# Dividing five groups' values by their sums after the value matmul, in a newly planned order

## The chip, the cores and the metric

The kernel runs on one core of a Trainium2 chip. The metric is the device time of one execution in microseconds (us); the number shown for a kernel is the median of three runs.

## The reference

Sparse attention in 32 heads, then a feed-forward layer on its output. S is 768, D is 64, the window 16, a block 32; there are 4 batches of 8 heads, 3072 tokens, 512 model and 2048 hidden columns.

```python
k_sum = k.reshape(B, H, nb, block, D).max(axis=3)
v_sum = v.reshape(B, H, nb, block, D).mean(axis=3)
scores_l = scale * q @ k^T, kept where |i - j| < window, else -1e9
scores_s = scale * q @ k_sum^T + log(block)
a = exp(scores_all - max);  a = a / (sum(a) + 1e-9)
attn = a @ concat(v, v_sum)
x = attn as (tokens, 512);  h = x @ w_in;  g = h * cos(h);  out = g @ w_out
```

The weights arrive in double precision, as pairs of 32-bit words, and the kernel rebuilds single precision from the bits.

## The kernel before

The 3072 tokens are eight blocks of 384. A block's attention is done in four groups, a to d, each a pair of heads; "b0" is group b of block 0. A group has six tiles of 64 queries for each of two heads, laid out as 128 rows (two half tiles) by six. Each tile sees 96 keys of its window and 24 block summaries, NK = 120 columns, so the scores of a group are 128 x 720. A column behind the 120 holds 1e-9, which the sum takes in.

Steps of a group, with the letters that the order uses: load q, k, v and the value summaries (q, k, v, m: the queue of SyncE, SP); turn q and k with PE and copy them to SBUF (tq, tk, cq, ck); key summaries (ks); masks into PSUM and scores on top (ms, sc, L556, L569); copy to SBUF (z); maximum (mx, L588, DVE); subtract it (su, L593, POOL); exponential (ex, L606, ACT); sum (sm, L609, DVE) and its reciprocal (iv, L614, DVE); multiply all exponentials by it (nm, L617, POOL); turn them with PE in two parts and copy them (tp, L626; cp); values (va, L670, PE); high part of x (xh) and what it leaves (xl, L356, DVE). From block 2 on the masks are added by DVE, and from c2 on the exponentials are turned by DVE in squares and put in place through DRAM (pt, po, pi) and not by PE.

Weights come in 16 slices w0 to w15, each 128 hidden columns: load (l), magnitude (ab, L388, ACT), clamp (cl, L393, DVE or POOL), three integer steps on DVE (sh, lb, fb, L399, L407, L415), high part (hi) and low part (lo, L356). The steps of the feed-forward part, s0 to s127, each take one block and one slice: 12 matmuls up (L714), the cosine gate on ACT and DVE, a high and a low part, 9 matmuls down (L770). s0 to s5 do block 0 with the first six slices, s6 to s21 block 1 with all, s22 to s31 the rest of block 0; then block after block. v0_0 and v0_1 are the value summaries of batch 0: load, halve (h, L259), sum (s).

The order of the instructions is written out in full as the string ORDER (lines 27 to 177): one list of tokens "who.step.banks.engine" for all engines. Each engine, and SP's queue of loads, runs its own tokens in that order and waits where an operand is not there. Buffers are few: slices share raw tiles (SLOTS) and two staging tiles, and all PSUM banks are named in the tokens.

Of the kernel before, what the change touches and what calls it, by code (L numbers as in the profile page):

```python
# [42 lines left out]
w8.sh.0.1 w3.hi.a b1.su a1.va.5 d1.z.0.v s1.tu c1.tp.0.7 w8.lb w3.lo.p a2.v d1.z.1.a c1.tp.1.3 s0.sq a2.tq.6 s1.re
c1.cp.1.a a1.xh.a s2.up.3 d1.mx s1.si c1.cp.0.a s0.ga d1.su w7.l w8.fb.0 s0.hi.a s1.sq c1.va.2 s0.lo.p w9.ab.1 s1.ga
w6.l s3.up.7 w8.hi.v s2.tu b2.q s1.hi.v d1.ex w9.cl.v s1.lo.p a1.xl s0.dh.0.1.4 s2.re w8.lo.p c1.xh.v s3.tu s0.dl
c1.xl s2.si s3.re s4.up.5 a2.cq.v v1_0.s.p d1.sm s2.sq s3.si s2.ga s1.dh w7.ab.0 d1.iv s2.hi.v d1.nm v1_1.l w9.sh.2.3
s1.dl s3.sq b1.ex s3.ga s2.lo.p d1.tp.0.6 w9.lb d1.tp.1.7 s2.dh w7.cl.p s4.tu b1.sm d1.cp.1.a s2.dl d1.cp.0.a s4.re
# [910 lines left out]
```

## Time and profile before

| | |
|---|---|
| median of 3 runs | 663.17 us (660.64 to 663.44) |
| profiled execution | 661.89 us |
| its span | 660.1 us |
| PE busy | 632.6 us (96%) |
| DVE, ACT, POOL busy | 449.7, 363.9, 221.8 us |

How to read it: a matmul record's time overlaps with the next one's, so the cost of a group of them is taken from the start of its first record to the start of what follows. A float32 matmul shows as two records. PEclk is the granted clock of PE: 1.00 is 2.4 GHz and 0.50 is 1.2 GHz. Waits name what came last before the engine went on.

### The profile page before, as it was taken

To read this page: it belongs to the slowest core of one execution; us is meant where nothing else is said; L and a number is where in the kernel's file an instruction comes from. 1 tells how busy PE (TensorE), PEld (TensorE's weight loads), DVE (VectorE), ACT (ScalarE), POOL (GpSimd) and SP (SyncE) were. 2 spreads that over 40 slices of the span, in tenths; PEclk is the share of its full clock that TensorE was granted. 3 is DMA by queue.
4 is the path that set the end of the run, shared out by engine and by line. 5 is a ranking of instruction groups with operands and counts; after the bars stand their busy time and mean duration, and the time that the engine had idled before them with its cause. 6 is when DMAs were issued, how large, how long until landed. Compare 5 with 4: busy or idle time off the path is not lost.

```text
span 660.1 us, 13282 instructions
## 1 busy us (share of the span) xinstructions
PE 632.6 (96%) x5141; PEld 560.2 (85%) x5141; DVE 449.7 (68%) x798; ACT 363.9 (55%) x640; POOL 221.8 (34%) x219
## 2 busy tenths in 40 slices
PE   6478999999999999999999999999999999999996
...
GB/s 224 259 271 203 276 15 223 169 109 71 55 122 85 91 124 132 127 59 114 111 107 135 147 98 97 114 43 85 115 163 104 92 94 70 5 1 17 16 17 48
DMA packets 167158, 72.68 MB, mean 110 GB/s; under 512 B 136824, under 2 KB 155832, under 8 KB 167096
## 3 DMA queue, kind: packets, MB, share of 16 engines
...
q8 instruction: 40, 0.66, 0.4%
q14 instruction: 22, 0.18, 0.1%
HBM read 53.72 MB, written 15.73 MB: 105 GB/s over the span
## 4 chain that ended last, share of the span: by engine, by line
PE 86%; DMA 5%; SPq 3%; POOL 2%; DVE 1%; issue 1%; ACT 1%; DVEq 0%; POOLq 0%; ACTq 0%
PE banks L770 39%; PE banks L714 39%; PE banks L569 4%; PE banks L670 3%; DMA late<-in_moe_w_out_dram 3%; DMA late<-in_v_dram 1%; SPq L456 1%; POOL w L356 1%; DMA late<-in_q_dram 1%; POOL gl L356 1%; SPq L493 1%; POOL stage L393 0%; ACT stage L388 0%; PE banks L556 0%; DVE m L588 0%
## 5 line engine op out<-in xcount | busy, mean ns | idle before, releaser
L714 PE MATMUL banks<-xh,w 128*128 128x384 f32 x1024 | 272.1, 337 | 0.1
L770 PE MATMUL banks<-w,gh 128*128 128x512 f32 x768 | 198.1, 393 | 0.2 <-ACT gh L350 0.2
L714 PEld LDWEIGHTS banks<-xh,w 128*128 128x128 f32 x1024 | 185.9, 188 | 2.8 <-ACT pt L350 0.4
L714 PE MATMUL banks<-xl,w 128*128 128x384 f32 x512 | 171.4, 335 | 0.0
L770 PEld LDWEIGHTS banks<-w,gh 128*128 128x128 f32 x768 | 142.6, 188 | 29.0 <-ACT gh L350 0.5
L724 ACT ACTIVATE t<-banks 128x384 int32<-128x384 f32 x128 | 62.5, 489 | 133.6 <-DVE gl L356 54.9
L356 POOL TENSOR_TENSOR gl<-t,gh 128x384 fp32r<-128x384 f32 x55 | 56.6, 1029 | 221.4 <-ACT gh L350 86.0
L770 PE MATMUL banks<-w,gl 128*128 128x512 f32 x384 | 109.8, 394 | 0.1
L727 DVE SCALAR_TENSOR_TENSOR t<-t,banks 128x384 f32<-128x384 int32 x128 | 70.0, 548 | 56.9 <-ACT t L724 56.2
L732 ACT ACTIVATE t<-t 128x384 f32<-128x384 f32 x128 | 66.7, 523 | 66.3 <-DVE t L727 66.0
L714 PEld LDWEIGHTS banks<-xl,w 128*128 128x128 f32 x512 | 96.1, 188 | 1.6
L739 DVE SCALAR_TENSOR_TENSOR t<-t,banks 128x384 f32<-128x384 f32 x128 | 69.3, 546 | 41.2 <-ACT t L735 41.0
L770 PEld LDWEIGHTS banks<-w,gl 128*128 128x128 f32 x384 | 71.1, 188 | 14.6 <-DVE gl L356 0.2
L593 POOL TENSOR_TENSOR sc<-sc,m 128x720 f32<-128x720 f32 x28 | 40.1, 1431 | 129.2 <-DVE m L588 129.2
L735 ACT ACTIVATE t<-t 128x384 f32<-128x384 f32 x128 | 65.8, 521 | 2.1
L617 POOL TENSOR_TENSOR sc<-sc,r 128x720 f32<-128x720 f32 x28 | 39.5, 1411 | 51.4 <-DVE r L614 50.3
L350 ACT CAST gh<-t 128x384 fp32r<-128x384 f32 x68 | 34.7, 510 | 33.2 <-PE banks L770 16.5
L356 DVE TENSOR_TENSOR gl<-t,gh 128x384 fp32r<-128x384 f32 x73 | 41.7, 572 | 12.6 <-ACT gh L350 6.5
L356 POOL TENSOR_TENSOR w<-stage,w 128x1024 fp32r<-128x1024 f32 x15 | 36.2, 2416 | 10.0 <-ACT w L350 8.6
L352 DVE CAST gh<-t 128x384 fp32r<-128x384 f32 x60 | 23.2, 386 | 22.2 <-PE banks L770 20.4
L580 DVE SCALAR_TENSOR_TENSOR sc<-banks,mask 128x360 f32<-128x360 f32 x48 | 24.4, 524 | 19.2 <-PE banks L569 19.0
L569 PEld LDWEIGHTS banks<-kd,qd 64*64 64x64 f32 x1344 | 28.4, 135 | 9.4 <-issue 6.7
(102 smaller groups left out, 620.7 us busy)
## 6 DMA issues: line engine op xcount, KB each, us to landing
...
```

Source lines behind the costliest of these rows:

```text
L350: eng.copy(out=out, in_=in_)
L356: eng.tensor_tensor(out=lo, in0=src, in1=hi.bitcast(F32), op=ALU.subtract)
L569: nc.tensor.matmul(out=self.sp[hh][s * QT : (s + 1) * QT, c, lo : lo + n], lhsT=self.qd[rows, t * QT : (t + 1) * QT], rhs=self.kd[rows, ke ...
L593: nc.gpsimd.tensor_tensor(out=self.sc, in0=self.sc, in1=self.m.unsqueeze(2).broadcast_to([P, U, NK]), op=ALU.subtract)
L617: nc.gpsimd.tensor_tensor(out=self.sc, in0=self.sc, in1=self.r.unsqueeze(2).broadcast_to([P, U, NK]), op=ALU.mult)
L714: nc.tensor.matmul(out=self.h, lhsT=w_of(name, self.f)[:, c * P : (c + 1) * P], rhs=x_of(self.blk, part, c), start=n == 0, stop=n == last,)
L724: nc.scalar.activation(out=self.t.bitcast(I32), in_=self.h, func=AF.Copy, scale=1.0 / TWO_PI)
L727: nc.vector.scalar_tensor_tensor(out=self.t, in0=self.t.bitcast(I32), scalar=-TWO_PI, in1=self.h, op0=ALU.mult, op1=ALU.add)
L732: nc.scalar.activation(out=self.t, in_=self.t, func=AF.Sin, scale=0.5)
L735: nc.scalar.activation(out=self.t, in_=self.t, func=AF.Square, scale=math.sqrt(2.0))
L739: nc.vector.scalar_tensor_tensor(out=self.t, in0=self.t, scalar=-1.0, in1=self.h, op0=ALU.add, op1=ALU.mult)
L770: nc.tensor.matmul(out=self.acc[i], lhsT=g[:, i * P : (i + 1) * P], rhs=w_of(name, self.f), start=self.first and n == 0, stop=self.last an ...
```

## The change

LATE marks five groups: a0, b0, c0, d0 and a1. For these the sum (sm) and the multiplication of all exponentials (nm) are gone. The exponentials are turned as they are, now 121 rows with the 1e-9 column (tp). The value matmuls change sides: the exponentials are the weights and the values move, so that the output has queries as rows and 64 columns for each of six pairs of tile and head; a second matmul beside each, with a column of ones as the moving side, writes the sum into a 65th column. The reciprocal is read from there (iv), DVE multiplies the values by it into a tile xq which all five share (xn), and three PE transposes bring the result back to the layout of x (tx). PMAX is empty, so what it selects is not used.

The second string of TURNS moves b2 to the way through squares and DRAM. Two clamps, w3's and w7's, go from POOL to DVE and one, w4's, from DVE to POOL, so that one is left on POOL. ORDER is new throughout; shown is the part up to the first step s0.

```diff
@@ ORDER and its constants
+PMAX = ""
+LATE = "11111000000000000000000000000000"
-TURNS = ("00000000011111111111111111111111", "00000000001111111111111111111111")
+TURNS = ("00000000011111111111111111111111", "00000000011111111111111111111111")
 ORDER = """
-b0.k a0.q a0.k c0.q c0.k b0.tk.0.0 d0.k b0.ks.0 a0.tq.1 b0.tk.1.2 v0_1.l b0.ks.1 a0.tk.0.3 a0.cq.v v0_0.l a0.tk.1.4
-b0.ck.0.v a0.ck.0.a a0.ks.0 a0.ms.5.6 a0.ck.1.a a0.ks.1 b0.q a0.sc c0.tk.0.7 a0.z.1.a a0.z.0.v w1.l c0.ck.0.a a0.mx
-d0.tk.0.1 c0.ks.0 a0.su c0.tq.0 c0.tk.1.3 d0.q c0.cq.a d0.tk.1.4 c0.ms.6.5 d0.ks.1 a0.ex v0_1.h.p c0.ks.1 c0.ck.1.v
-w0.l d0.ks.0 c0.sc a0.sm c0.v c0.z.1.a v0_0.h.v b0.tq.7 c0.z.0.a b0.ms.0.3 b0.ck.1.a a0.iv v0_0.s.p b0.cq.a v0_1.s.v
-d0.ck.0.a b0.sc w1.ab.0 c0.mx c0.m d0.tq.5 b0.z.1.a w1.cl.v c0.su d0.ms.2.1 b0.z.0.a w2.l w1.sh.6.7 d0.cq.a d0.ck.1.a
-d0.sc w1.lb a0.nm c0.ex a0.v d0.z.1.a w1.fb.1 a0.tp.0.3 d0.z.0.a a0.tp.1.0 w0.ab.0 a0.m d0.mx w1.hi.a w0.cl.v d0.su
-d0.m c0.sm w0.sh.4.5 w5.l w1.lo.p c0.iv w2.ab.0 w0.lb c1.m a0.cp.0.a w2.cl.v c0.nm d0.ex b1.q w0.fb.1 a0.cp.1.a w3.l
-a0.va.1 d0.sm w0.hi.a d1.m w2.sh.6.7 w0.lo.p c0.tp.0.2 c1.q d0.iv w5.ab.0 w2.lb b1.tq.3 a1.q a0.xh.a d0.nm c0.tp.1.0
-w2.fb.1 c0.cp.0.a d0.v c0.cp.1.a w5.cl.v w2.hi.a c0.va.2 a0.xl w2.lo.p d0.tp.0.6 c0.xh.a w5.sh.4.5 w4.l d0.tp.1.7 a1.m
-b0.mx w3.ab.0 a1.tq.0 w5.lb b0.su a1.v a1.cq.a a1.ms.1.0 w5.fb.1 w3.cl.p b0.ex b0.m d0.cp.0.a a1.sc b0.sm b1.cq.a
-c1.tq.6 d0.cp.1.a c0.xl a1.z.1.a d0.va.3 b0.iv w3.sh.4.5 b0.nm a1.z.0.a b1.m c1.ms.7.2 d0.xh.a a1.mx c1.cq.a d1.q
-w4.ab.0 c1.sc w3.lb a1.su b0.v b0.tp.0.0 w5.hi.a b0.tp.1.1 d0.xl w4.cl.v c1.z.0.a c1.v b0.cp.0.a w4.sh.6.7 c1.z.1.a
-b1.ms.3.0 b0.cp.1.a v1_0.l c1.mx a1.ex w8.l w4.lb c1.su b0.va.2 b1.sc a1.sm b0.xh.a w5.lo.p c1.ex d1.tq.1 b0.xl
-b1.z.1.a a2.q a1.iv s0.up.2 w4.fb.0 b1.z.0.a a1.nm w3.fb.1 w4.hi.a a1.tp.0.0 d1.cq.a w4.lo.v w9.l d1.ms.3.6 s0.tu
...
+b0.k a0.k v0_0.l a0.q c0.k b0.tk.0.0 d0.k a0.tk.0.1 b0.tk.1.2 c0.q a0.ck.0.a a0.ks.0 b0.ck.0.v v0_0.h.p b0.ks.0 v0_1.l
+b0.ks.1 a0.tq.3 a0.tk.1.4 a0.ms.5.6 a0.ck.1.a a0.ks.1 b0.q v0_0.s.p a0.cq.v b0.ck.1.v a0.sc w1.l c0.tk.0.7 a0.z.1.a
+a0.z.0.v c0.tk.1.1 a0.mx c0.ck.1.a d0.q c0.ck.0.v a0.su c0.tq.0 c0.ks.1 d0.tk.0.4 c0.cq.a d0.tk.1.3 w0.l d0.ck.0.v
+c0.ms.2.6 a0.ex c0.ks.0 v0_1.h.p d0.ks.0 c0.sc a0.v d0.ks.1 b0.tq.5 b0.ms.1.0 b0.cq.a v0_1.s.v c0.z.0.a c0.z.1.a
+a0.tp.0.7 a0.tp.1.2 b0.sc a1.q w1.ab.0 c0.mx w2.l d0.tq.6 w1.cl.v c0.su d0.cq.a w1.sh.4.5 d0.ck.1.a b0.z.0.a d0.ms.6.3
+a0.cp.0.a w1.lb d0.sc a0.m w0.ab.0 w1.fb.1 d0.z.1.a c0.m a0.cp.1.a w0.cl.v d0.z.0.a w1.hi.a d0.mx w5.l w0.sh.4.5 c0.ex
+w1.lo.p c0.v w0.lb b1.q a0.va.1 d0.su w2.ab.1 w0.fb.0 c1.q w2.cl.v w0.hi.a w2.sh.2.3 d0.ex w0.lo.p c0.tp.0.7 w3.l
+a0.iv w5.ab.1 w2.lb c0.tp.1.6 d0.m c0.cp.0.a w5.cl.v c0.cp.1.a w2.fb.0 b1.tq.7 d0.v c0.va.6 a0.xn w2.hi.a w5.sh.4.5
+w4.l a0.tx.2 d0.tp.0.3 b0.z.1.a w2.lo.p a1.tq.1 d0.cp.0.a b0.mx a0.xh.a a1.ms.0.3 w5.lb b0.v a1.cq.a w3.ab.1 b0.su
+d0.tp.1.1 a1.sc a0.xl w5.fb.0 b0.m d0.cp.1.a c1.tq.2 b0.ex d0.va.1 w3.cl.v b1.cq.a w8.l a1.z.0.a c0.iv w3.sh.4.5
+a1.z.1.a c1.ms.7.0 c1.cq.a v1_0.l d0.iv w4.ab.1 a1.mx b0.tp.0.3 d1.q b0.tp.1.2 c1.sc d0.xn b0.cp.1.a w4.cl.p b1.m
+w3.lb b0.cp.0.a d0.tx.1 c1.z.0.a b0.va.2 d0.xh.a c0.xn a1.m c1.z.1.a d0.xl c0.tx.3 b0.iv b1.ms.7.6 c1.mx c0.xh.a b1.v
+w5.hi.a a1.su c0.xl b1.sc w4.sh.0.1 c1.su a1.ex c1.v d1.tq.3 b0.xn b1.z.1.a w4.lb b0.tx.2 w5.lo.p a1.tp.0.6 a1.v
+b0.xh.a d1.cq.a b0.xl c1.ex w4.fb.1 s0.up.3 w7.l b1.z.0.a v1_0.s.p w3.fb.0 w4.hi.a c1.m d1.ms.2.7 a1.cp.0.a w4.lo.v
...
@@ -305,6 +309,8 @@
     KW = WINDOW + S + WINDOW
     qd0 = const.tile([P, TB], F32, name="qd")
+    ones = const.tile([P, 1], F32, name="ones")
+    nc.vector.memset(ones, 1.0)
     kmax = const.tile([P, NB // 2, BLOCK // 2], F32, name="kmax")
     kd = [const.tile([P, KW + NB], F32, name=f"kd{i}") for i in range(NPAIR)]
     vn0 = [const.tile([NK, U, P], F32, name=f"vn{i}") for i in range(2)]
@@ -440,6 +446,10 @@
             self.squares, self.moved = (t[blk * NG + pr : blk * NG + pr + 1] == "1" for t in TURNS)
+            self.late = LATE[blk * NG + pr : blk * NG + pr + 1] == "1"
+            self.rows = NK + 1 if self.late else NK
+            self.pmax = int(PMAX[blk * NG + pr : blk * NG + pr + 1] or "0")
             self.kT, self.pT, self.pt, self.pts = {}, {}, {}, None
         def load_heads(self, t, src, squares):
@@ -549,6 +559,7 @@
         def score_banks(self, two):
             self.sp = [bank(i)[:, : QC * NK].rearrange("p (c n) -> p c n", c=QC) for i in two]
+            self.first_bank = two[0]
         def place_masks(self, *two):
             self.score_banks(two)
@@ -585,6 +596,16 @@
         def maximum(self):
             m = self.m = att.tile([P, U], F32, name="m", bufs=2)
+            if self.pmax:
+                i = self.first_bank
+                nc.vector.tensor_reduce(
+                    out=m.rearrange("p (c h) -> p h c", h=2),
+                    in_=banks[:, i : i + 2, : QC * NK].rearrange("p h (c n) -> p h c n", n=NK),
+                    axis=AX.X, op=ALU.max,
+                )
+                if self.pmax == 2:
+                    nc.vector.tensor_scalar_mul(m, m, -1.0)
+                return
             nc.vector.tensor_reduce(
                 out=m, in_=self.sc, axis=AX.X, op=ALU.min if self.fused else ALU.max
             )
@@ -595,8 +616,16 @@
             )
         def exp(self):
-            self.r = att.tile([P, U], F32, name="r", bufs=2)
-            if self.fused:
+            if not self.late:
+                self.r = att.tile([P, U], F32, name="r", bufs=2)
+            if self.pmax == 2:
+                for u in range(U):
+                    c, h = divmod(u, 2)
+                    nc.scalar.activation(
+                        out=self.sc[:, u, :], in_=self.sp[h][:, c, :], func=AF.Exp, bias=self.m[:, u : u + 1],
+                        accum_out=self.r[:, u : u + 1],
+                    )
+            elif self.fused:
                 for u in range(U):
                     nc.scalar.activation(
                         out=self.sc[:, u, :], in_=self.sc[:, u, :], func=AF.Exp, bias=self.m[:, u : u + 1],
@@ -609,7 +638,11 @@
             nc.vector.tensor_reduce(out=self.r, in_=self.all[:, :, : NK + 1], axis=AX.X, op=ALU.add)
         def inverse(self):
-            if self.fused:
+            if self.late:
+                self.r = att.tile([P, U], F32, name="r", bufs=2)
+                nc.vector.reciprocal(out=self.r, in_=self.xw[:, :, D])
+                return
+            if self.fused or self.pmax == 2:
                 nc.vector.tensor_scalar_add(self.r, self.r, 1e-9)
             nc.vector.reciprocal(out=self.r, in_=self.r)
@@ -621,15 +654,15 @@
         def turn_p(self, j, i):
             lo, hi = ((0, 4), (4, U))[j]
-            pT = self.pT[j] = bank(i)[:NK, : (hi - lo) * P].rearrange("p (t n) -> p t n", t=hi - lo)
+            pT = self.pT[j] = bank(i)[: self.rows, : (hi - lo) * P].rearrange("p (t n) -> p t n", t=hi - lo)
             for t in range(lo, hi):
-                nc.tensor.transpose(out=pT[:, t - lo, :], in_=self.sc[:, t, :], identity=ident)
+                nc.tensor.transpose(out=pT[:, t - lo, :], in_=self.all[:, t, : self.rows], identity=ident)
         def place_p(self, j, eng):
             lo, hi = ((0, 4), (4, U))[j]
             if self.pts is None:
                 self.pts = att.tile([P, U * P], F32, name="pt")
-            pt = self.pts[:NK].rearrange("p (t n) -> p t n", t=U)
+            pt = self.pts[: self.rows].rearrange("p (t n) -> p t n", t=U)
             copy(eng, pt[:, lo:hi, :], self.pT[j])
             for t in range(lo, hi):
                 self.pt[t] = [pt[:, t, s * QT : (s + 1) * QT] for s in range(2)]
@@ -662,6 +695,19 @@
         def values(self, i):
+            if self.late:
+                self.xw = bank(i)[:, : U * (D + 1)].rearrange("p (u n) -> p u n", u=U)
+                for t in range(U):
+                    c, s = divmod(t, 2)
+                    for hh in range(2):
+                        p, to = self.pt[2 * c + hh][s], self.xw[s * QT : (s + 1) * QT, 2 * c + hh]
+                        nc.tensor.matmul(
+                            out=to[:, :D], lhsT=p[:NK], rhs=self.vn[:, t, hh * D : (hh + 1) * D],
+                            start=True, stop=True,
+                        )
+                        nc.tensor.matmul(out=to[:, D:], lhsT=p, rhs=ones[: self.rows], start=True, stop=True)
+                return
             self.xps = bank(i)[:, :TB]
             for t in range(U):
                 c, s = divmod(t, 2)
@@ -671,6 +717,18 @@
                         out=self.xps[rows, t * QT : (t + 1) * QT], lhsT=self.vn[:, t, rows],
                         rhs=self.pt[2 * c + hh][s], start=True, stop=True,
                     )
+        def divide(self):
+            nc.vector.tensor_tensor(
+                out=self.xq.rearrange("p (u n) -> p u n", u=U), in0=self.xw[:, :, :D],
+                in1=self.r.unsqueeze(2).broadcast_to([P, U, D]), op=ALU.mult,
+            )
+        def turn_x(self, i):
+            self.xps = bank(i)[:, :TB]
+            for c in range(QC):
+                cols = slice(c * P, (c + 1) * P)
+                nc.tensor.transpose(out=self.xps[:, cols], in_=self.xq[:, cols], identity=ident)
         def x_part(self, part):
             return x_of(self.blk, part, self.pr)
@@ -844,7 +902,7 @@
         return got if len(shape) == 2 else got.rearrange("p (c n) -> p c n", c=shape[1])
     n_v, n_k, n_s = U * P, KC * P, U * NKP
-    x1 = [xp.tile([P, 2 * TB], F32, name=f"x1_{i}", tag=t) for i, t in enumerate(("xh01", "xl01", "xh11"))]
+    x1 = [xp.tile([P, 2 * TB], F32, name=f"x1_{i}", tag=t) for i, t in enumerate(("xh01", "xl01", "xh11", "xl11"))]
     qd1 = carve(late[2], 2 * n_k, P, TB)
     kn = [carve(late[2], 0, P, KC, P), carve(late[2], n_k, P, KC, P), carve(x1[2], 0, P, KC, P), None]
     qn = [
@@ -862,6 +920,7 @@
     for t in vn_b:
         nc.gpsimd.memset(t[:, U - 1, :], 0.0)
+    Group.xq = carve(x1[3], 0, P, TB)
     groups = [
         [Group(0, i, vn_a[i], sc[i], qn[i], kn[i], (qd0, qd1)[i % 2]) for i in range(NG)],
         [Group(1, i, vn_b[i], sc[i], qn[i], kn[i], (qd0, qd1)[i % 2]) for i in range(NG)],
@@ -905,7 +964,7 @@
             q="load_q", k="load_k", v="load_v", m="load_vs", tq="turn_q", tk="turn_k", qt="square_q", kt="square_k", pt="square_p", po="move_out", pi="move_in", cq="place_q",
             ck="place_k", ks="k_summaries", ms="place_masks", sc="scores", z="scale", mx="maximum",
             su="less_max", ex="exp", sm="sums", iv="inverse", nm="normalize", tp="turn_p", cp="place_p",
-            va="values", xh="x_high", xl="x_low",
+            va="values", xn="divide", tx="turn_x", xh="x_high", xl="x_low",
         ),
         Summaries: dict(l="load", h="halve", s="sum"),
         Slice: dict(
```

## Rows read from the trace of the kernel before

**Rows 1.** The page, parts 1 and 2: busy time, and tenths in 40 slices.

```profile
span 660.1 us, 13282 instructions
...
PE 632.6 (96%) x5141; PEld 560.2 (85%) x5141; DVE 449.7 (68%) x798; ACT 363.9 (55%) x640; POOL 221.8 (34%) x219
...
PE   6478999999999999999999999999999999999996
```

**Rows 2.** Busy time by windows: PE, PEld, DVE, ACT, POOL, PEclk, DMA share, GB/s.

```profile
0.00:10.00 10.00, 5.12 (x18) 3.89 (x19) 3.79 (x10) 2.24 (x3) 4.91 (x34) 1.00 0.88 201
10.00:20.00 10.00, 7.56 (x123) 5.39 (x123) 6.29 (x11) 4.10 (x9) 4.02 (x3) 1.00 1.06 290
...
30.00:40.00 10.00, 4.80 (x47) 3.81 (x49) 9.68 (x13) 6.45 (x10) 7.94 (x5) 0.50 0.85 245
40.00:50.00 10.00, 8.19 (x105) 5.98 (x102) 7.85 (x10) 5.36 (x11) 8.65 (x4) 0.74 0.85 230
...
22.93:58.74 35.81, 22.52 (x338) 16.30 (x337) 31.29 (x37) 22.78 (x39) 25.95 (x15) 0.76 0.80 211
```

**Rows 3.** PE's waits from 0 to 100 us: total, times, longest.

```profile
PE banks L502 <- DMA late<-in_q_dram: 6.6, 3, 2.4
PE banks L670 <- ACT pt L350: 5.6, 2, 5.4
...
PE banks L670 <- DMA vn<-in_v_dram: 2.3, 1, 2.3
```

**Rows 4.** PE in order of time: start, duration, line, records, idle time before.

```profile
11.11 1.09 PE L569 MATMUL banks<-kd,qd 64*64 64x96 f32 x48
...
56.71 0.92 PE L670 MATMUL banks<-pt,vn 120*64 120x64 f32 x24 [2.27 <-DMA vn<-in_v_dram]
...
58.88 0.43 PE L714 MATMUL banks<-xh,w 128*128 128x384 f32 x1
...
61.06 0.60 PE L626 MATMUL banks<-ident,sc 128*120 128x128 f32 x4
61.50 1.38 PE L556 MATMUL banks<-mask,ident 128*128 128x360 f32 x4
62.71 0.38 PE L626 MATMUL banks<-ident,sc 128*120 128x128 f32 x2
63.02 1.09 PE L569 MATMUL banks<-kd,late 64*64 64x96 f32 x48
64.04 0.45 PE L714 MATMUL banks<-xh,w 128*128 128x384 f32 x1
...
66.36 0.92 PE L670 MATMUL banks<-pt,late 120*64 120x64 f32 x24
67.21 0.65 PE L626 MATMUL banks<-ident,late 128*120 128x128 f32 x4
```

**Rows 5.** DVE in order of time.

```profile
22.93 0.70 DVE L393 TENSOR_SCALAR stage<-stage 128x1024 f32<-128x1024 f32 x1 [0.31 <-ACT stage L388]
...
28.80 0.90 DVE L609 TENSOR_REDUCE r<-late 128x6 f32<-128x726 f32 x1
...
30.75 0.18 DVE L614 RECIPROCAL r<-r 128x6 f32<-128x6 f32 x1
...
58.18 0.56 DVE L356 TENSOR_TENSOR xl<-banks,xh 128x384 fp32r<-128x384 f32 x1 [1.14 <-ACT xh L350]
```

**Rows 6.** POOL in order of time.

```profile
15.20 2.36 POOL L259 TENSOR_TENSOR late<-late 96x1024 f32<-96x1024 f32 x1
...
24.83 1.38 POOL L617 TENSOR_TENSOR sc<-sc,r 128x720 f32<-128x720 f32 x1
...
44.18 3.62 POOL L393 TENSOR_SCALAR stage<-stage 128x1024 f32<-128x1024 f32 x1
```

**Rows 7.** ACT in order of time: w5's magnitude.

```profile
37.20 1.15 ACT L388 ACTIVATE stage<-late 128x1024 f32<-128x1024 f32 x1 [1.99 <-DMA late<-in_moe_w_out_dram]
```

**Rows 8.** SP's queue in order of time: the first two loads of b0's v.

```profile
52.91 1.26 SPq L477 DMA_DIRECT2D vn<-in_v_dram  x2
```

More of the change, by code (lines that the diff above doesn't have):

```diff
@@ L43 @@
[L43 to L47, printed above, removed]
@@ new lines @@
+s25.ga d2.su c2.pt.0 s23.dl s25.hi.a d2.ex c2.po s24.dh s25.lo.v b3.q s27.re s24.dl s27.si s25.dh d2.sm d2.iv d2.nm
+s28.up.3 s21.ta.0.0.v s26.tu s27.sq s26.re s21.st.0 c2.pi s26.si s29.up.1 s26.sq s26.ga s27.ga s26.hi.v s30.up.2
+s26.lo.v s28.tu s28.re d2.pt.0 s28.si s25.dl s28.sq s26.dh d2.po s27.hi.a v2_0.l s27.lo.v s21.st.1 s28.ga s26.dl
+s28.hi.a a3.sc.5.0 s30.tu s28.lo.p c2.va.3 a3.z.0.v s29.tu s30.re s31.up.5 c2.xh.a d2.pi b3.qt s30.si s30.sq s30.ga
+s27.dh c3.q s29.re a3.z.1.v s29.si s27.dl s29.sq s29.ga s28.dh a3.v a3.mx s28.dl s29.hi.v a3.m s30.hi.a d2.va.2
@@ new lines @@
+s51.re s52.up.1 s50.lo.v b4.kt.1 a4.z.0.v c4.k b4.qt s53.up.3 a4.z.1.v s52.tu s51.si s52.re s47.st.2 s51.sq b4.ks.1
+s52.si a4.v s51.ga s49.dh a4.mx b4.ks.0 a4.su b4.m s49.dl s51.hi.a s52.sq b4.sc.0.6 s51.lo.v a4.ex c4.q s50.dh
+b4.z.0.v c4.kt.0 c4.kt.1 s50.dl s47.ta.1.1.a a4.sm s51.dh s53.tu d4.k a4.iv b4.z.1.v a4.nm s51.dl s52.ga s53.re
+s54.up.0 s52.hi.a a4.pt.0 s53.si b4.mx a4.po s55.up.5 c4.ks.1 b4.su s53.sq c4.ks.0 c4.qt s53.ga s56.up.6 s52.lo.v
+s53.hi.a s54.tu s53.lo.v s54.re s55.tu s52.dh s54.si s55.re a4.pi s54.sq s55.si s54.ga s52.dl b4.ex s54.hi.v s53.dh
@@ new lines @@
+d7.sc.6.1 s101.sq b7.va.2 d7.z.0.v d7.z.1.v s103.up.0 d7.m d7.mx s101.ga d7.su c7.pi s101.hi.v s104.up.6 d7.ex
+s101.lo.v s102.hi.v s105.up.1 s103.tu s103.re d7.sm s103.si s101.dh s102.lo.v s101.dl s103.sq s102.dh s105.tu b7.xh.a
+b7.xl s102.dl s103.ga c7.va.5 s105.re s106.up.2 c7.xh.a s105.si s103.hi.a s105.sq s103.lo.v s107.up.0 c7.xl s104.tu
+s104.re s104.si s104.sq s103.dh s104.ga s105.ga s103.dl s104.hi.v s105.hi.v s104.dh s104.lo.v s106.tu s105.lo.v
+s104.dl s106.re d7.iv s108.up.5 s106.si d7.nm s106.sq s107.tu s107.re s109.up.6 s106.ga s107.si d7.pt.1 s106.hi.a
```

250 lines of the change are left out of this document (120 added, 130 removed).

## The prediction

> **What bounds the kernel now.** I read the page first [rows 1]: TensorE (PE) is busy for 632.6 of 660.1 us, and its line of tenths shows where the other 27.5 us lie: in the first four slices of 16.5 us and in the last one. From the fifth slice on PE has work in every slice, so from there the kernel is a row of matmuls whose length is given, and a faster VectorE (DVE), ScalarE (ACT) or GpSimd (POOL) buys nothing there. The windows come next [rows 2]: from 30 to 40 us PE is busy for 4.80 of 10 us and its granted clock is 0.50 (1.2 GHz); DVE is busy for 9.68 in the same stretch. So the opening is held by DVE and by what feeds it, not by PE. PE's waits in the first 100 us [rows 3] are late loads of q (6.6 us), a copy of the transposed exponentials that comes late on ACT (5.6 us, 5.4 of it in one piece) and a load of v (2.3 us). Last, PE's order of time [rows 4]: the first matmul of the feed-forward part (L714, step s0) starts at 58.88 us, right behind group b0, the last of block 0 to be ready; behind it PE has next to no gap. That gives the frame: the end moves by what s0's start moves, plus PE work that is added behind s0, plus any new gap behind it, with about 5 us of copies and stores after the last matmul.
>
> **Part 1: the late division, work that goes.** In five groups (a0, b0, c0, d0, a1) the sum over the exponentials goes (DVE, L609, 0.90 us each [rows 5]) and so does the multiplication of all 720 exponentials (POOL, L617, 1.38 us each [rows 6]): 4.5 us of DVE and 6.9 of POOL. The chain of one group loses these two steps between the exponential and the transposes.
>
> **Part 1: work that comes, on PE.** A group's values (L670, 24 records) take 0.85 us, 66.36 to 67.21 [rows 4]. After the change there are 24 records more, with the same 64 columns of weights but one moving column. Lower bound: the scores (L569), 48 records with 64-column weights and 96 or 24 moving columns, take 1.02 us from 63.02 to 64.04 [rows 4], 21 ns a record, so 24 cost 0.51. Upper bound: they cost like the 64-column records, 0.85; if the new order of the halves (four records on one half of the output before the other, instead of two) also took away the overlap of the halves, the old part would go up to 24 x 57 ns = 1.37, where 57 ns is 64 columns at the rate of the masks (L556: 4 x 360 columns in 1.21 us, taken as 0.89 ns a column with its start [rows 4]). I take 0.51, since one column is nearer to 24 than to 64. Then come three transposes back: four take 0.44 us from 61.06 to 61.50 [rows 4], three 0.33. So a group costs PE 0.84 more (0.84 to 1.70), five groups 4.2 (to 8.5).
>
> The Trainium skill speaks against the cheap value: "TensorEngine Tiling (Array Packing)", Instruction Overhead, says that a matmul with one free column has the latency of one with 60. No run here shows a one-column matmul. By that rule the ones would cost 0.85 a group, four groups 1.4 us more on PE before s0, and the forecast below would be 660.2.
>
> **Part 1: work that comes, on DVE.** The division (384 numbers out of PSUM) is nearest to the x rest at L356, 0.56 [rows 5]; the reciprocal, 0.18 [rows 5], stays but moves behind the values. Upper bound for the division 0.90, the reduction over 720. So DVE gains 0.90 - 0.56 = 0.34 a group (0 to 0.34). All five groups share one buffer for the divided values (xq), so each division waits for the transposes of the one before.
>
> **Where these lie.** The work of four groups stands before s0. a1's stands behind it, on the full PE: +0.84; against it a1's first transposes move ahead of s0 (0.44) and b2's six transposes leave PE (0.66, the price of four scaled up): -0.26, to +0.6 at the upper price. b2's transposes become one DVE instruction and a round trip by five DMAs, at a place where DVE is two thirds busy over the span [rows 1] and PE has other groups and steps: 0; without that cover it is the latency of one trip. The clamp: w3 and w7 go from POOL to DVE, w4 from DVE to POOL: 3.62 us on POOL against 0.70 on DVE [rows 5, 6]. Before s0 that is one for one; behind it POOL loses a1's multiplication and one clamp, 5.0 us, and DVE gets 0.70. All else in the order counts as 0 behind s0: PE had no wait of over 0.5 us there.
>
> **Part 2: the new order, the head.** SyncE's queue now has block 0's v sums (two loads, 768 KB) before a0's q. At the 201 to 290 GB/s of the first two windows [rows 2] that is 2.6 to 3.8 us. So a0's scores, at 11.11 before [rows 4], come at about 14, and so does everything that follows in PE's order. But the first weight slice, w1, has the same loads ahead of it, so its magnitude on ACT can start when it did, and DVE's stream of slices begins when c0's maximum is done. Both steps of the first v sum are now on POOL ahead of a0's subtraction (a halving is 2.36 [rows 6]), and the sum of the other stands on DVE before c0's maximum. DVE started its stream at 22.93 [rows 5]; I take 24.1 (22.9 if the v work fits the idle time, 25.5 if most of the delay of q comes through).
>
> **The new order, DVE's floor.** From 22.93 to 58.74 DVE was busy for 31.29 us and idle for 4.52 [rows 2]. Counting both orders, this stretch loses the sums of c0, d0, b0 and a1 (3.6), gains four divisions (2.24) and one reciprocal (0.18), swaps one clamp for another: 31.29 - 1.2 = 30.1. With no idle time at all b0's last step would end at 24.1 + 30.1 = 54.2.
>
> **The new order, PE's way there.** c0's values wait for c0's copy, which stands on ACT behind w5's magnitude, which waits for w5's load (37.20 before [rows 7]). Between w0 and w5 SyncE issues 11 DMAs instead of 14, at 0.63 us each (two in 1.26 [rows 8]): 35.3. Magnitude 1.15 [rows 7] and two copies of about 0.5 give 37.3 for c0's values. From there to s0 PE has, at full clock, three values (1.36 each), four times three transposes (0.33), transposed exponentials of d0, b0 and half of a1 (1.8), three q (0.33), masks (1.21) and scores (1.02) of three groups: 4.1 + 1.3 + 1.8 + 1.0 + 3.6 + 3.1 = 14.9 us. In the old windows the clock was 0.50 from 30 to 40 and 0.74 from 40 to 50 [rows 2], about 7.5 us at 1.2 GHz behind 37.3. Time at half speed does half the work: 37.3 + 14.9 + 3.7 = 55.9. What takes away the rest of the old wait: b0's v, issued at 52.91 [rows 8] and the 2.3 us wait of [rows 3], has six load steps (13 DMAs, 8 us) less ahead of it.
>
> **The sum.** The later of 54.2 (DVE) and 55.9 (PE) is 55.9, 3.0 us before 58.88; behind s0 -0.3 to +0.6, taken as +0.1. The profiled execution took 661.89 us (its span 660.1 and 1.8 around it): 661.9 - 3.0 + 0.1 = 659.0. The median of the three runs, 663.17, is 1.3 above the profiled one, the lowest 1.3 below it.
>
> **The rivals.** (B) PE's waits vanish and DVE alone decides: the stream starts at 22.9 and runs without a gap, 53.0, so 5.9 before: 656.1. For it: DVE's four old waits for sums and POOL clamps go. Against: new waits for PE (reciprocals stand in DVE's order and wait for values). (C) Slower: PE becomes the bound of the opening at 1.2 GHz. Place: c0's values to s0. Price: half of each us at the low clock; 37.3 + 14.9 + h/2 passes 58.88 when h is over 13.4 us, that is when the clock stays low until 50.7. With h = 19 it is 61.7: 664.8. For it: PE still has its hole from about 31 to 37, in front of which the clock fell before; against: the work behind it is denser. (D) The edit does what it says, but off the path: DVE starts at 24.1, does 30.1, and is idle for 4.52 as before, now behind the reciprocals and one xq: 58.7, so 661.8.
>
> **How the numbers follow.** Forecast 0.42 (657.3 to 660.6: DVE's floor to the dear ones), B 0.22, C 0.18, D 0.18. A measurement here can tell about 0.5% from no change, 3.3 us: under 658.6 is faster, over 665.2 slower by profile, and C reaches from 663 to 670. Faster: B and 0.16 of the forecast, 0.38. Slower: most of C with gaps behind s0 added, 0.16. Same: the rest, 0.46. The range leaves out the far ends of B and C: 655.5 to 665.0.
>
> **What would show it.** Right: s0's first matmul at 54 to 57.5 us, PE full behind it; a group's values at 1.2 to 1.5 us; the division at 0.5 to 0.6; no PE wait for b0's v. Wrong in its steps: s0 at 58 or later with DVE idle in front of reciprocals or divisions (D), or with PE busy at 1.2 GHz from 38 to 55 (C); values at 1.7 or more (the dear ones); PE waits behind s0 that sum up to over 1 us (the rest of the order is not neutral).

## The result and the profile after

The median is 665.67 us after (663.59 to 667.09, 10 runs) against 663.13 before, the ratio 1.0042 [1.0028, 1.0055]: slower by a little under 3 us, and 0.7 us above the upper end of the range. The profiled execution took 666.1 us, 4.2 more than that of before; its s0 starts at 64.43 us, where 55.9 was forecast and 58.88 was the old place [rows 4]. So the sign was wrong, and in this pair of profiles all of the loss lies ahead of s0: from s0 to the end of the span it is 599.9 us after and 601.2 before.

Lines have moved with the diff: L512 (old L502) turns q, L705 and L709 are the late values and their ones, L731 the turning back, L659 (old L626) that of the exponentials, L567 and L580 masks and scores, L772 and L828 up and down, L394 (old L388) the magnitude.

The page of after, against [rows 1]:

```profile
span 664.3 us, 13551 instructions
...
PE 639.9 (96%) x5270; PEld 569.7 (86%) x5270; DVE 445.6 (67%) x791; ACT 366.1 (55%) x645; POOL 211.4 (32%) x218
```

PE has 7.3 us more of busy time and 3.1 less of idle time (24.4 against 27.5); their sum is the 4.2. The part that was meant to be the gain, less idle PE, came. The part that was priced too low, PE's own time, is larger.

Windows of after, columns as in [rows 2]; the last two are in 20 us:

```profile
30.00:40.00 10.00, 4.70 (x54) 4.52 (x54) 7.93 (x9) 4.73 (x7) 6.06 (x3) 0.67 0.96 224
40.00:50.00 10.00, 8.01 (x65) 6.90 (x65) 6.39 (x8) 5.13 (x9) 3.71 (x2) 0.50 1.17 276
50.00:60.00 10.00, 10.00 (x215) 8.63 (x214) 6.43 (x12) 6.10 (x13) 4.98 (x2) 0.98 0.95 211
60.00:80.00 20.00, 19.41 (x249) 16.62 (x248) 19.46 (x28) 17.74 (x30) 12.60 (x10) 1.00 0.95 260
80.00:100.00 20.00, 20.00 (x141) 17.03 (x140) 18.15 (x29) 16.11 (x29) 15.06 (x12) 1.00 0.40 80
```

DVE, busy for 9.68 of 10 us from 30 to 40 before, is down to 7.93, and to 6.4 in the next two windows, while PE goes up to 8.01 at a clock of 0.50 and then to 10.00. The opening has changed its bound, from DVE to PE. Behind 60 us DVE is at 97% and 91%.

PE's waits from 0 to 100 us, against [rows 3]. One of them is new, 7.0 us for value summaries ahead of a0's values, at the place where PE waited 5.4 us for ACT's copy before. (The profile names the summaries of c0, x, whose load stands right behind a0's; in the run warm below the same wait is for a0's own, vn.) The waits for q are 5.4 us in total against 6.6, but the longest is 3.4 against 2.4.

```profile
PE banks L705 <- DMA x<-vs: 7.0, 1, 7.0
PE banks L525 <- DMA late<-in_k_dram: 5.5, 2, 4.8
PE banks L512 <- DMA late<-in_q_dram: 5.4, 2, 3.4
```

PE in order of time, against [rows 4]. The fence names the first record of each step; a late group's values are alternating pieces of L705 and L709.

```profile
35.30 0.44 PE L705 MATMUL banks<-vn,pt 120*64 120x64 f32 x2 [6.99 <-DMA x<-vs]
...
42.11 0.87 PE L512 MATMUL banks<-ident,late 128*128 128x128 f32 x3 [1.99 <-DMA late<-in_q_dram]
42.91 0.48 PE L705 MATMUL banks<-x,pt 120*64 120x64 f32 x2
...
46.12 0.90 PE L731 MATMUL banks<-ident,x 128*128 128x128 f32 x3
...
52.36 0.33 PE L705 MATMUL banks<-x,pt 120*64 120x64 f32 x2
...
54.22 1.48 PE L567 MATMUL banks<-mask,ident 128*128 128x360 f32 x4
...
59.63 0.55 PE L731 MATMUL banks<-ident,x 128*128 128x128 f32 x3
60.01 1.38 PE L567 MATMUL banks<-mask,ident 128*128 128x360 f32 x4
...
64.43 0.45 PE L772 MATMUL banks<-xh,w 128*128 128x384 f32 x1 [0.52 <-ACT late L518]
```

c0's values start at 42.91 (37.3 forecast), a late group at full clock takes 1.86 us (52.36 to 54.22; 1.36 forecast) and at 1.2 GHz 3.21 (42.91 to 46.12). From 42.91 to s0 PE is idle for 0.6 us in all, so the row of its work ends in s0.

### The profile page after: what moved, and what is told of

It reads as the page before. It is cut to its first block, busy times and chain, and to the rows that moved or that the text cites. A ratio compares the mean times of both kernels' runs of the same rounds, so it can differ in the third digit from the quotient of the medians.

```text
span 664.3 us, 13551 instructions
## 1 busy us (share of the span) xinstructions
PE 639.9 (96%) x5270; PEld 569.7 (86%) x5270; DVE 445.6 (67%) x791; ACT 366.1 (55%) x645; POOL 211.4 (32%) x218
## 4 chain that ended last, share of the span: by engine, by line
PE 94%; DMA 3%; SPq 1%; POOL 1%; DVE 1%; issue 0%; ACT 0%; DVEq 0%
PE banks L772 41%; PE banks L828 40%; PE banks L580 5%; PE banks L716 3%; DMA late<-in_q_dram 2%; PE banks L567 1%; DMA late<-in_moe_w_out_dram 1%; PE banks L705 1%; PE banks L659 1%; PE banks L512 1%; SPq L466 0%; PE banks L731 0%; PE banks L709 0%; POOL late L263 0%; DVE vs L273 0%; POOL late L614 0%
## 5 line engine op out<-in xcount | busy, mean ns | idle before, releaser
L772 PE MATMUL banks<-xh,w 128*128 128x384 f32 x1024 | 272.4, 337 | 0.5 <-ACT late L518 0.5
L828 PE MATMUL banks<-w,gh 128*128 128x512 f32 x768 | 198.5, 393 | 0.0
L772 PEld LDWEIGHTS banks<-xh,w 128*128 128x128 f32 x1024 | 186.0, 188 | 3.3 <-ACT late L518 0.7
L772 PE MATMUL banks<-xl,w 128*128 128x384 f32 x512 | 171.4, 335 | 0.0
L828 PEld LDWEIGHTS banks<-w,gh 128*128 128x128 f32 x768 | 142.4, 188 | 28.7
L362 POOL TENSOR_TENSOR gl<-t,gh 128x384 fp32r<-128x384 f32 x53 | 53.8, 1016 | 200.8 <-DVE gh L358 78.0
L828 PE MATMUL banks<-w,gl 128*128 128x512 f32 x384 | 109.8, 394 | 0.0
L772 PEld LDWEIGHTS banks<-xl,w 128*128 128x128 f32 x512 | 96.1, 188 | 1.9
L828 PEld LDWEIGHTS banks<-w,gl 128*128 128x128 f32 x384 | 71.1, 188 | 14.4
L356 ACT CAST gh<-t 128x384 fp32r<-128x384 f32 x73 | 37.3, 511 | 55.7 <-DVE t L797 35.2
L650 POOL TENSOR_TENSOR sc<-sc,r 128x720 f32<-128x720 f32 x25 | 35.4, 1415 | 94.6 <-DVE r L647 75.4
L362 DVE TENSOR_TENSOR gl<-t,gh 128x384 fp32r<-128x384 f32 x75 | 41.7, 558 | 27.9 <-PE banks L828 18.4
L580 PEld LDWEIGHTS banks<-kd,qd 64*64 64x64 f32 x1344 | 28.2, 134 | 8.7 <-issue 5.9
L591 DVE SCALAR_TENSOR_TENSOR sc<-banks,mask 128x360 f32<-128x360 f32 x48 | 24.4, 523 | 16.1 <-PE banks L580 16.1
```

Of the source, the lines that this page charges most:

```text
L356: eng.copy(out=out, in_=in_)
L362: eng.tensor_tensor(out=lo, in0=src, in1=hi.bitcast(F32), op=ALU.subtract)
L580: nc.tensor.matmul(out=self.sp[hh][s * QT : (s + 1) * QT, c, lo : lo + n], lhsT=self.qd[rows, t * QT : (t + 1) * QT], rhs=self.kd[rows, ke ...
L650: nc.gpsimd.tensor_tensor(out=self.sc, in0=self.sc, in1=self.r.unsqueeze(2).broadcast_to([P, U, NK]), op=ALU.mult)
L772: nc.tensor.matmul(out=self.h, lhsT=w_of(name, self.f)[:, c * P : (c + 1) * P], rhs=x_of(self.blk, part, c), start=n == 0, stop=n == last,)
L828: nc.tensor.matmul(out=self.acc[i], lhsT=g[:, i * P : (i + 1) * P], rhs=w_of(name, self.f), start=self.first and n == 0, stop=self.last an ...
```

## The experiments

Two theories from these rows. **P**: PE's own work, dearer than priced and begun at 1.2 GHz, is the new bound of the opening. **Q**: the new order of the loads brings w2, w5, a0's summaries and q too late, so PE's row starts late. Both can hold; the runs size them. The start of c0's values and those of the first up-matmuls of s0 and s5 are of the profiled execution, the ratio is of all runs.

| kernel | c0's values | s0 | s5 | ratio to before, 95% |
|---|---|---|---|---|
| before | 39.26 | 58.88 | 84.95 | 1 |
| after | 42.91 | 64.43 | 89.42 | 1.0042 [1.0028, 1.0055] |
| late_old | 44.21 | 67.48 | 93.41 | 1.0129 [1.0091, 1.0168] |
| order_only | 49.85 | 82.03 | 108.04 | 1.0353 [1.0326, 1.0380] |
| no_ones | 42.58 | 59.87 | 85.37 | 1.0030 [1.0009, 1.0050] |
| warm | 41.95 | 60.63 | 90.50 | 1.0038 [1.0011, 1.0066] |
| warm_a2q | 41.06 | 59.38 | 85.58 | 1.0032 [1.0013, 1.0052] |
| q_first | 40.74 | 61.86 | 88.28 | 1.0029 [1.0010, 1.0049] |
| loads | 39.53 | 60.61 | 87.66 | 1.0050 [1.0033, 1.0067] |
| loads2 | 40.65 | 60.23 | 86.76 | 1.0019 [1.0004, 1.0034] |
| loads3 | 38.09 | 59.16 | 85.75 | 1.0034 [1.0017, 1.0052] |
| before_b0v | 41.21 | 59.26 | 86.18 | 1.0013 [0.9997, 1.0029] |
| before_warm | 39.18 | 59.75 | 85.27 | 1.0017 [0.9999, 1.0034] |
| before_both | 40.13 | 58.81 | 88.54 | 1.0032 [1.0015, 1.0049] |

**Each half alone: late_old and order_only.** late_old is the changed kernel in the order of before, with TURNS as before and iv, xn and tx put in ahead of each late group's xh; order_only keeps the new order and makes no group late.

```diff
late_old:   ORDER = that of before; -a0.sm -a0.iv -a0.nm  +a0.iv +a0.xn +a0.tx.1 (ahead of a0.xh; b0, c0, d0, a1 alike)
order_only: -LATE = "11111000..."  +LATE = "00000000..."  +a0.sm +a0.iv +a0.nm (ahead of a0.tp; the others alike)
```

> The late division alone, in the order of the kernel before: for a0, b0, c0, d0, a1 the sum and the multiplication are taken out, and reciprocal, division and transposes back stand right ahead of the copy to x; loads, b2 and clamps as before. Theory P (PE is the bound of the opening, and the added PE work, 1.0 us of ones and 0.3 to 0.5 us of transposes a group at full clock, double at 1.2 GHz, makes s0 late): s0 at 62 to 65 us instead of 58.9, 665 to 668 us. Theory Q (the new order of the loads makes s0 late; the added work fits PE's idle time): s0 at 58 to 60, 661.5 to 664.

> The new order alone: no group divides late; for the five groups sum, reciprocal and multiplication stand ahead of the transposes of the exponentials, and the copy to x right behind the values. Theory P: PE's opening is 5 to 8 us shorter, s0 at 58 to 60, 659 to 662 us. Theory Q: the loads are as late as in the changed kernel, s0 at 62 to 65, 664 to 668 us.

The late division in the order of before costs 1.3% and puts s0 at 67.48, later than either theory had it; c0's values start at 44.21, 5 us later than before. So the new order isn't the cause of the loss as a whole: it takes back two thirds of what the late division costs in the old one. How much of the 1.3% comes from an order that wasn't planned for it is not shown. The reverse, order_only, misses both theories by far and doesn't tell them apart. The largest of PE's waits there are for POOL's multiplications (L650), which that order no longer has room for:

```profile
PE banks L659 <- POOL late L650: 14.6, 2, 9.7
PE banks L659 <- POOL sc L650: 12.3, 3, 4.3
```

**The price of the ones: no_ones.** The kernel leaves out the sums.

```diff
-nc.tensor.matmul(out=to[:, D:], lhsT=p, rhs=ones[: self.rows], start=True, stop=True)
-nc.vector.reciprocal(out=self.r, in_=self.xw[:, :, D])
+nc.vector.reciprocal(out=self.r, in_=self.xw[:, :, 0])
```

> The changed kernel without the matmuls with a column of ones; the reciprocal is taken of a column of values, so the sum over the exponentials is left out. Theory P: the three groups behind 42 us lose 1.0 us each, c0 at 1.2 GHz 1.4: s0 3 to 4 us earlier, at 60.5 to 61.5, 662 to 663 us. Theory Q: s0 waits for the loads, less than 1 us, 665 us or more.

PE of no_ones in order of time:

```profile
42.58 1.60 PE L705 MATMUL banks<-x,pt 120*64 120x64 f32 x24
44.12 0.90 PE L730 MATMUL banks<-ident,x 128*128 128x128 f32 x3
...
49.46 0.97 PE L705 MATMUL banks<-x,pt 120*64 120x64 f32 x24
50.36 1.48 PE L567 MATMUL banks<-mask,ident 128*128 128x360 f32 x4
```

A group without ones takes 0.90 at full clock and 1.54 at 1.2 GHz. The ones cost 0.96 (1.86 - 0.90) and 1.67 (3.21 - 1.54). c0's at the low clock and d0's and b0's at the full one make 3.6 of the 4.6 us by which s0 is earlier; c0's values started 0.3 earlier, and the rest goes with a clock of 0.67 from 40 to 50 us instead of 0.50. So the ones put s0 back by 3.6 us, as P has it. The median did not follow: 664.93, where P had 662 to 663.

**The clock: warm, and the same in before.** Ten unused mask matmuls ahead of a0's values and six ahead of b1.tq; in warm_a2q a2's q is also loaded earlier.

```diff
+x.warm.10.1 (ahead of a0.va)  +x.warm.6.5 (ahead of b1.tq)
+a2.q behind a1.v (warm_a2q alone)
```

> The changed kernel with matmuls that nothing uses put into PE's two holes: ten of the mask (6.4 us) ahead of a0's values, six (3.8 us) ahead of b1's transposes of q. They only keep PE at work, so that the granted clock stays at 1.00. Theory P: what PE does from 42 to 50 us at 1.2 GHz takes half the time, s0 4 us earlier, at 60 to 61, 661 to 663 us. Theory Q, or DVE as the bound: s0 moves by less than 1 us, 665 us or more.

> The filled holes of the run before, with a2's q issued six steps earlier in SyncE's queue. In that run s0 came 3.8 us earlier, but PE then waited 2.6 us for a2's q in front of its transposes and the clock fell again, and the time was given back. If a2's q is what gives it back: no wait there, 661 to 662.5 us. If the rest behind s0 (DVE, POOL, w3) can't follow an earlier s0: a wait comes elsewhere, 664 to 665 us.

> The kernel before with unused mask matmuls in PE's three holes of the opening: 8 ahead of a0's values, 4 ahead of the turning of b1's q, 2 ahead of that of a1's q. The clock should then be granted at 1.00 from 30 to 50 us instead of 0.50 and 0.74. Theory P (PE bounds the opening only since the change; before, DVE, copies and loads held it): s0 at 58.0 to 59.0 and the ratio to before 0.999 to 1.001, while the same edit in the changed kernel brought s0 forward by 3.8 us. Rival (the low clock costs both kernels alike): s0 3 us earlier, 55.9, ratio 0.996.

Windows of warm, and of before_warm, where the same is done to the kernel before (8, 4 and 2 matmuls in its three holes):

```profile
30.00:40.00 10.00, 9.10 (x76) 6.40 (x75) 7.75 (x10) 5.65 (x7) 6.09 (x3) 1.00 0.99 240
40.00:50.00 10.00, 9.73 (x167) 7.70 (x166) 8.85 (x11) 6.93 (x14) 3.71 (x2) 1.00 1.13 275
```

```profile
30.00:40.00 10.00, 7.85 (x73) 5.21 (x71) 9.66 (x12) 5.99 (x10) 8.95 (x5) 1.00 0.86 249
40.00:50.00 10.00, 8.98 (x149) 6.00 (x146) 8.37 (x11) 6.86 (x13) 8.66 (x4) 1.00 0.85 224
```

Both run the stretch from 30 to 50 us at 1.00. In the changed kernel s0 comes 3.8 us earlier, 1.0 of it because c0's values start earlier; in the kernel before s0 doesn't come earlier at all (59.75 against 58.88). There PE still waits 2.38 us for b0's v and the clock falls once more around that (0.71 from 50 to 60): b0's values, b1's scores and d1's q take 1.48, 1.79 and 0.55 us instead of 0.85, 1.02 and 0.30, so at full clock s0 would have been at about 58.1, a gain of 0.8 at most. PE in order of time, in before_warm and then in before, where s0 follows at 59.75 and 58.88:

```profile
55.93 1.55 PE L670 MATMUL banks<-pt,vn 120*64 120x64 f32 x24 [2.38 <-DMA vn<-in_v_dram]
57.41 1.86 PE L569 MATMUL banks<-kd,late 64*64 64x96 f32 x48
59.20 0.90 PE L502 MATMUL banks<-ident,qn 128*128 128x128 f32 x3
```

```profile
57.56 1.09 PE L569 MATMUL banks<-kd,late 64*64 64x96 f32 x48
58.58 0.55 PE L502 MATMUL banks<-ident,qn 128*128 128x128 f32 x3
```

This tells P from its rival best: PE's rate bounds the opening only since the change. The end gains less than s0. In the profiled execution of warm PE then waits 2.59 us for a2's q; that execution was the slowest of its ten (670.36 us, the median 664.70), so the wait need not be there in the others.

```profile
72.22 0.87 PE L512 MATMUL banks<-ident,qn 128*128 128x128 f32 x3 [2.59 <-DMA qn<-in_q_dram]
```

warm_a2q has no such wait, and its ratio is still only 0.001 (0.7 us) below that of after, which the intervals don't tell apart; its profiled execution was the fastest of its ten (662.99 us, the median 664.13).

**The loads: q_first, loads, loads2, loads3.**

```diff
q_first: +a0.q ahead of v0_0.l
loads:   +a0.m behind a0.v  +a1.q behind b1.q  +a2.q behind a1.v
loads2:  loads  +c1.q behind d0.v  +b1.tq behind c0.va  +w5.ab, w5.cl behind c0.cp  +x.warm.2.1, x.warm.5.5 ahead of a0.va, c0.va
loads3:  loads2, but +x.warm.3.2 ahead of w2.sh in place of x.warm.5.5
```

> The changed kernel with one load moved: a0's q is issued ahead of the first v sum's load, not behind it. Theory H (the late head, 4 us in a0's scores, is passed on to s0): a0's scores at 12 instead of 15.2, s0 3 us earlier, 662 to 663.5 us. Theory P (PE is bound from 42 us on by its work and by 1.2 GHz; the head is waited out in the hole ahead of a0's values): s0 within 1 us of 64.4, 665 to 666 us.

> The changed kernel with three loads moved in SyncE's queue: a0's value summaries right behind a0's v (they stood behind a1's q and w2), a1's q behind b1's q, a2's q six steps earlier. Theory Q (late loads start PE's bound stretch late): a0's values at 29 to 31 instead of 35.3, w2 and w5 some 2 us earlier, c0's values at 40 to 41 instead of 42.9, s0 at 61.5 to 62.5, 662 to 664 us. Theory P alone: PE's hole only moves to the place ahead of b1's q, the clock falls all the same, s0 within 1 us of 64.4, 665 to 666.

> All of these together: the three moved loads, c1's q behind d0's v, b1's transposes of q behind c0's values, c0's copies ahead of w5's magnitude on ACT, and PE's holes filled (two unused matmuls of the mask ahead of a0's values, five ahead of c0's). Theory P with Q: c0's values at 36 to 39, s0 at 56 to 59, 657 to 660.5 us, the first of these kernels below the kernel before. If DVE's stream of weight slices is the bound by then (it needs until about 59): s0 at 59 to 60.5, 660.5 to 662.5 us.

> The changed kernel with the orders of loads of loads2 (a0's summaries behind its values, a1's q behind b1's, a2's q behind a1's values, c1's q behind d0's values, c0's copies ahead of w5's magnitude, b1's q turned behind c0's values), but the unused matmuls in front of c0's values go to an earlier place where they hold up nothing: 2 ahead of a0's values, 3 ahead of c0's transposes. c0's values then wait for c0's copies alone. Theory P plus Q (late loads start PE's stretch, PE's work then sets its length): c0's values at 38.1 instead of 40.65 and s0 at 57.5 to 58.3 instead of 60.23, if the clock stays at 1.00 over the gap ahead of c0's values; if it falls there, s0 at 59 to 60.5. With 602.5 us behind s0 as in the other variants the median is 661.5 to 662.5, ratio 0.998 to 1.000. Rival (DVE's chain decides s0): s0 stays at 59.5 to 60.5 with PE waiting for DVE or ACT, ratio 1.002.

Theory Q holds too for s0. In the four kernels where the clock is low behind the start of c0's values (after, q_first, loads and loads3) the way from there to s0 is 21.5, 21.1, 21.1 and 21.1 us: the loads set when it starts (in loads3 4.8 us earlier, s0 5.3), PE's work and its clock how long it is. In warm_a2q, at 1.00 throughout, it is 18.3. In q_first P alone, which had s0 within 1 us of 64.4, was wrong: the late head does reach s0. In loads3 the clock did fall ahead of c0's values (0.84 and 0.82 from 30 to 50), which its expectation put at 59 to 60.5. But s5 doesn't follow: between s4 and s5 after takes 7.84 us, loads3 9.46. There PE waits for one DVE step of the cosine gate, and DVE had been waiting for a weight slice, here in DVE's and in PE's order of time in loads3:

```profile
74.85 0.69 DVE L400 TENSOR_SCALAR stage<-stage 128x1024 f32<-128x1024 f32 x1 [2.09 <-ACT stage L395]
```

```profile
82.53 0.84 PE L660 MATMUL banks<-ident,late 128*120 128x128 f32 x6 [1.21 <-DVE t L798]
```

**What bounded before: before_b0v and before_both.**

```diff
before_b0v:  +b0.v, b0.m ahead of a1.m
before_both: before_b0v and before_warm
```

> The kernel before with one edit of its order: b0's values (and its summaries) are loaded ahead of a1's and b1's summaries, a1's values and d1's q. Before, PE waited 2.27 us for b0's values right ahead of s0. Frame theory (the end moves by what s0's first matmul moves): s0 at 56.6 to 57.0 instead of 58.88, the median 1.9 to 2.3 us down, ratio to before 0.997. Rival (what is won ahead of s0 is given back behind it, since DVE and a2's q don't come earlier): s0 at 56.8 as well, but PE waits of 1 to 2 us between s0 and s5, ratio 0.999 to 1.001. Rival that the values aren't what is late last: s0 stays at 58.5 to 58.9, with a wait for another operand in that place.

> The two edits together in the kernel before: b0's values early and the holes filled. If PE's clock becomes a bound once b0's values are there, s0 comes another 0.5 to 1.7 us earlier than with the values alone (55.2 to 56.3) and the ratio is 0.995 to 0.997. If DVE's chain is what is next late, s0 is that of the values alone, 56.6 to 57.0, and the ratio 0.997 to 0.998.

The 2.27 us wait for b0's v [rows 4] is gone, and s0 stays: PE waits for DVE instead, in before_b0v twice, once ahead of b1's masks and once at s0.

```profile
54.11 1.48 PE L556 MATMUL banks<-mask,ident 128*128 128x360 f32 x4 [1.32 <-DVE xl L356]
...
59.26 0.45 PE L714 MATMUL banks<-xh,w 128*128 128x384 f32 x1 [1.32 <-DVE xl L356]
```

The frame theory had s0 at 56.6 to 57.0 and got this wrong; the load of v was late beside DVE's chain, not instead of it. In before_both the clock is 1.00 from 40 to 60 and s0 still stands at 58.81, behind d1's q, which the edit had moved behind b0's v:

```profile
58.53 0.52 PE L502 MATMUL banks<-ident,qn 128*128 128x128 f32 x3 [2.09 <-DMA qn<-in_q_dram]
```

So in this opening one late operand stands close behind another (v, DVE's xl, q), while in after PE waits for next to nothing from 42.91 on. None of the twelve is faster than before; before_b0v and before_warm can't be told from it. In the profiled execution of before_b0v a0's values start 3.0 us later than in that of before (35.58 against 32.58), ahead of the edit: the opening differs by that much from one execution to the next, so s0 and s5 in the table carry some us of chance, and the medians are to be believed over them.

## Why the prediction was wrong, step by step

- **What bounds the kernel now**: right for the opening of before. DVE and late loads held it, and filling PE's holes or loading b0's v earlier moved nothing.
- **DVE's floor**: the stream started at 25.10 (24.1 forecast, 25.5 its upper bound), the division takes 0.55 (0.56 forecast), and from there to the last x rest ahead of s0 DVE was busy for 30.04 us (30.1 forecast). But that took 39.48 us, 9.4 of them idle, so the floor was right and not what counted. Rival D's sign came with it: DVE stood idle for 1.87, 0.91 and 0.79 us in front of reciprocals and a division. There it was DVE that waited for PE, as in the second of these rows, while PE went on, so D's cause is not this one. The last row is the window, columns as in [rows 2].

```profile
25.10 0.68 DVE L399 TENSOR_SCALAR stage<-stage 128x1024 f32<-128x1024 f32 x1
...
57.88 0.56 DVE L722 TENSOR_TENSOR x<-banks,r 128x384 f32<-128x384 f32 x1 [0.91 <-PE banks L731]
```

```profile
25.10:64.58 39.48, 29.29 (x448) 24.53 (x448) 30.04 (x39) 23.29 (x41) 20.24 (x11) 0.78 0.98 224
```

- **The place of c0's values: the largest miss, 5.6 us** (42.91 against 37.3). "11 DMAs instead of 14, at 0.63 us each" failed: it took three DMAs off the old time, as if the 11 that are left cost what they cost before. In the trace of before the 14 stand between the two rows below, from 19.15 to 31.31: 0.87 us each. In after 11 take from 19.96 to 33.11: 1.20 each, so fewer DMAs took 1.0 us more. SP's queue of before, then of after:

```profile
18.30 0.85 SPq L375 DMA_DIRECT2D late<-in_moe_w_out_dram  x1
...
31.31 0.46 SPq L371 DMA_DIRECT2D late<-in_moe_w_in_dram  x1
```

```profile
19.61 0.35 SPq L381 DMA_DIRECT2D late<-in_moe_w_out_dram  x1
20.08 2.44 SPq L487 DMA_DIRECT2D vn<-in_v_dram  x2
22.56 0.51 SPq L495 DMA_DIRECT2D vn<-in_v_dram  x1
23.18 2.05 SPq L466 DMA_DIRECT2D late<-in_q_dram  x2
25.33 2.23 SPq L377 DMA_DIRECT2D late<-in_moe_w_in_dram  x1
27.61 1.76 SPq L381 DMA_DIRECT2D late<-in_moe_w_out_dram  x1
29.46 1.82 SPq L503 DMA_DIRECT2D vn<-vs  x2
31.39 1.60 SPq L503 DMA_DIRECT2D x<-vs  x2
33.11 0.45 SPq L377 DMA_DIRECT2D late<-in_moe_w_in_dram  x1
```

  By the forecast w5's load would have been issued at 29.4 (31.31 - 1.89); it came 3.7 us later, 0.8 from a queue that was late at w0 already and 2.9 from the dearer DMAs. Another 0.8 went by from there to the magnitude (6.72 us against 5.89). So w5's magnitude ran at 39.83 instead of 35.3, the two copies for c0 behind it ended at 41.7, and PE did b1's q first, which had come late too (1.99 of wait): 4.5 + 1.1. ACT in order of time:

```profile
39.83 1.11 ACT L394 ACTIVATE stage<-late 128x1024 f32<-128x1024 f32 x1 [2.00 <-DMA late<-in_moe_w_out_dram]
40.85 0.85 ACT L356 COPY pt<-banks 121x512 f32<-121x512 f32 x2
```

  The 0.63 itself is no cause: with the 0.87 of this stretch the three that went would have put w5 earlier still.
- **PE's full-clock work, 2.3 to 3.0 us**. From 42.91 to 64.43 it is 21.5 us, of which 0.6 idle. The clock was 0.50 until about 50.4 (0.70 from 48 to 52), so 7.5 us, as forecast, cost 3.75. What is left is 17.2 against 14.9. Three late values at 1.86 instead of 1.36 are 1.5 of it; four turnings back at about 0.4 instead of 0.33 another 0.3; the masks, at 1.31 instead of 1.21 (54.22, 60.01), about as much. warm_a2q gives the same without a subtraction: at 1.00 throughout PE was busy for 17.87 us of the 18.32 from c0's values to s0 (first row below), 3.0 more than forecast, and the low clock then cost after 3.2. The second row is of after.

```profile
41.06:59.38 18.32, 17.87 (x338) 14.58 (x337) 14.99 (x21) 12.08 (x25) 11.04 (x6) 1.00 1.02 225
```

```profile
48.00:52.00 4.00, 4.00 (x58) 2.93 (x57) 3.03 (x5) 3.38 (x7) 0.00 (x0) 0.70 1.15 272
```

- **The ones: 0.96, not 0.51.** The choice "nearer to 24 than to 64" columns failed: the cost was above the 64-column 0.85, inside the bounds (0.51 to 1.37). The Trainium skill, "TensorEngine Tiling (Array Packing)", Instruction Overhead, gives a one-column matmul the latency of a 60-column one. Its side was right, and the measurement goes 0.11 us beyond the 64-column price. The sum that the prediction gives by that rule, 660.2, is off by 0.2: by its own terms it is 660.4 with four groups, 660.0 with the three behind c0's place.
- **Rival C had the mechanism**, PE as the bound of the opening at 1.2 GHz, at the place named, and 664.8 is within 1 us of the median. That the number comes so near is luck: in it s0 is at 61.7 by 9.5 us of low clock, and s0 was at 64.43 by 3.2 to 3.75. Its deciding point (h over 13.4) wasn't reached: the clock stayed low until 50.4, close to the 50.7 that it names, but PE's stretch began only at 42.91, so h was 7.5. What took PE past 58.88 was its late start and its dearer work. C was given 0.18 and weighed on the clock alone; the bounds of the other two terms were never added together in it.
- **Behind s0**: +0.1 forecast, -1.3 in the profile, 1.1 of it between s0 and s5; behind 90 us PE waits for nothing in after and for 0.2 us in before. But the frame that the end moves by what s0's start moves holds only as long as s0 is late. Where s0 came 2.6 to 5.3 us earlier, s5 came 1.1 to 4.1 earlier (in warm not at all, which lost it to q) and the ratio fell by 0.0023 (1.5 us) at most, in loads2, where the intervals still overlap; in loads it rose. In no_ones, warm and loads3 s0 came where the theory had it or earlier, and the medians lie 1.7 to 2.2 us above the upper end of what was expected with it. So that the late s0 is what costs the median its 2.5 us is not shown. DVE, "two thirds busy" over the span, is at 97% from 60 to 80 us in after, and PE waits about 1.2 us for it between s4 and s5 in loads, loads2 and loads3: that a faster VectorE buys nothing there was read from an average. But DVE's share isn't what gives the gain back: in loads3 it is 85% (17.03 of 20 us).
- **Still open**: why no variant gets below the median of before although s0 is within 0.3 to 1.8 us of its place in six variants of the changed kernel. Two waits show above; in loads3 s5 is 0.8 us late and the profiled span 2.4 us longer than that of before, so some more is lost behind s5. One profile of each can't part this from chance.
